# The last token group's second product: 26 block products instead of 28

## The chip, the cores and the metric

The kernel runs on one core of a Trainium2 chip. The metric is the device time of one execution in microseconds (us). A core has TensorE (PE, the matrix engine; PEld is its loading of weights), VectorE (DVE), ScalarE (ACT), GpSimd (POOL) and SyncE (SP, which issues transfers). Each works through a queue of its own in order and waits on semaphores for the others.

## The reference

Two stages, in float32. The first is an mLSTM cell over 4 batches, 8 heads, 768 steps and a head size of 40; its outcome is laid out as a matrix x of 3072 tokens by 320. The second, which the change touches, is

```
h = x @ w_in                    # 3072x320 @ 320x2048
g = np.maximum(0.01 * h, h)     # leaky relu
out = g @ w_out                 # 3072x2048 @ 2048x320
```

## The kernel before

**Stages.** The sequence is cut into 6 chunks of 128 steps. A chunk gives one token group: 4 blocks (one a batch) of 128 tokens. The loop at the end of the kernel goes over the groups; for each it runs a list of units that `ff_units` returns, and between them pieces of the cell for the next chunk. The order of issue on PE, DVE, ACT and POOL is the order in which the program is written. For the last group (g = 5) there is no cell work left: only its units run.

**First product.** `fast_firsts(g)` gives 14 units. They compute the transposed activations `acts` (2048 rows as 16 slices f of 128, by 512 tokens of the group) with a 2x2 scheme of Strassen's kind, 7 products for two values n each. A product is a set of matmuls with 64 weight rows and 256 columns at line 1036 into a pair of accumulator banks. For most units DVE then adds the pair of banks to `acts` (line 1065, 128x512 each), and ACT applies the leaky relu (line 1061). Units 8 to 13 in the last group finish with such a pair of adds.

**Second product.** `fast_units(g)` gives 14 units: again a 2x2 scheme with 7 products, once for each n of two. `acts` is seen as 2x2 blocks (two halves of the slices f, two token blocks), `w_out` as 2x2 blocks (two halves of the slices, two halves of 160 columns). One block product is 8 matmuls, each with 128x128 of `acts` as weights and 128x160 of `w_out` moving, summed in one accumulator bank (line 929). Sums of `acts` are made in place on DVE (lines 950, 955, 969, 983; 128x1024 each). Sums of the weights were made once, early (lines 231 to 234): `t2`, `t3`, `t4` in the tile `raw`, and one in place, so that the second column half of `w_out`'s first 8 slices no longer holds `w_out` itself but its difference to the first half. The results are put together by copies on ACT (lines 951, 966, 974, 981), adds on POOL (lines 967, 975, 977) and adds on DVE (lines 959, 988, 993), and sent off by SP (line 95, called from `send`). In the last group two token blocks go out in halves of 160 columns, the others whole.

**Banks.** Accumulator banks come from two pools of 4, `psf` (tag "mm") and `psc` (tag "c"). Products of both stages take `psf` in turn; `psc` serves the cell and is idle in the last group.

Of the kernel before, what the change touches and what calls it, by code (L numbers as in the profile page):

```python
# [8 lines left out]
F32 = mybir.dt.float32  # L9
# [3 lines left out]
AF = mybir.ActivationFunctionType  # L13
ALU = mybir.AluOpType
# [4 lines left out]
def kernel(  # L19
# [26 lines left out]
    nc = tc.nc  # L46
    B, H, S, D = q.shape
    P = 128
    BH = B * H
    NB = S // P  # L50
    NS = B * NB
    Dm, FF = moe_w_in.shape
    PR = H // 2
    DP = 64
    D1 = D + 1
# [24 lines left out]
    wk = ctx.enter_context(tc.tile_pool(name="wk", bufs=2))  # L80
    psf = ctx.enter_context(tc.tile_pool(name="psf", bufs=4, space=PSUM))
    psc = ctx.enter_context(tc.tile_pool(name="psc", bufs=4, space=PSUM))
# [18 lines left out]
    sync, by_act = queues = Ordered(nc.sync), Ordered(nc.scalar)  # L101
# [37 lines left out]
    NL = 4  # L139
    NR = 2  # L140
    EAB = 2
    kn = consts.tile([P, NL, H, DP], F32, name="kn")
    qn = consts.tile([P, NL, H, DP], F32, name="qn")
    S_t = [consts.tile([P, 2, H, DP], F32, name=f"S{n}") for n in range(NL)]
    S_v = [t[:].rearrange("p u h (k d) -> p u h k d", d=QW) for t in S_t]
    rb_t = [consts.tile([P, 3, RW], F32, name=f"rb{n}") for n in range(NR)]
    xb = consts.tile([P, PR * TB, QW], F32, name="xb")
    w_all = consts.tile([P, NL, H * P], F32, name="w")
    acts = consts.tile([P, NF, GT], F32, name="acts")
# [41 lines left out]
    QN = NF // 4  # L191
    QC = 4 * P
    WC = KC * 2 * P
    w_in = consts.tile([P, QN, WC], F32, name="w_in")
    w_out = consts.tile([P, NF, Dm], F32, name="w_out")

    def f_of(r, j):
        n, e = divmod(j, 2)
        return 4 * n + 2 * r + e

    def w_row(r, slot, j):
        n, e = divmod(j, 2)
        at = (e * KC + slot) * P
        return w_in[DP * r : DP * (r + 1), n, at : at + P]
# [10 lines left out]
    raw_l = raw_t[:].bitcast(F32)  # L215
    KH = NF // 2
    NH = Dm // 2
    low_w, high_w = w_out[:, :KH, :], w_out[:, KH:, :]
# [6 lines left out]
    p1_at = [raw_l[:, at + 12 * P + 2 * HT + n * NH :][:, :NH] for n in range(2)]  # L225
# [640 lines left out]
    def ff_units(g):  # L866
        xT = st["xT", g]

        def rows(j, ph, cols, slots):
            for slot in slots:  # L870
                for r in range(2):
                    nc.tensor.matmul(  # L872
                        ph[r][:, cols], lhsT=w_row(r, slot, j), rhs=xT[DP * r : DP * (r + 1), slot, cols],
                        start=(slot == 0), stop=(slot == KC - 1),
                    )

        def relu(j, ph, cols):
            for r in range(2):
                f = f_of(r, j)
                nc.scalar.activation(acts[:, f, cols], ph[r][:, cols], AF.Prelu, alpha=0.01)  # L880

        def half(j, h):
            ph = [psf.tile([P, GT], F32, name=f"ph{r}", tag="mm") for r in range(2)]
            cols = ts(h, GT // 2)
            rows(j, ph, cols, range(KC))
            relu(j, ph, cols)

        po = {}

        def part(n, m):  # L890
            if m == 0:
                po[n] = psf.tile([P, Dm], F32, name="po", tag="mm")
            for f in range(m * NF // 4, (m + 1) * NF // 4):
                nc.tensor.matmul(  # L894
                    po[n][:], lhsT=acts[:, f, ts(n, P)], rhs=w_out[:, f, :], start=(f == 0), stop=(f == NF - 1),
                )
            if m == 3:
                if n < 2:
                    y = wk.tile([P, Dm], F32, name="y")[:]
                else:  # L900
                    y = wk.tile([P, H, D1], F32, name="hn")[:].rearrange("p h d -> p (h d)")[:, :Dm]
                nc.scalar.copy(y, po[n][:])
                sync.dma_start(out[n * S + g * P : n * S + (g + 1) * P, :], y)

        if g == 0:

            ins = [(j, h) for j0 in range(0, NF // 2, 4) for h in range(2) for j in range(j0, j0 + 4)]
            ins = ins[:2] + ins[4:6] + sorted(ins[2:4] + ins[6:])
            return [lambda j=j, h=h: half(j, h) for j, h in ins] + [
                lambda n=n, m=m: part((n + 2) % B if m == 3 else n, m) for m in range(4) for n in range(B)  # L910
            ]
        return fast_firsts(g) + fast_units(g)

    def quarter(n, i, k):

        return acts[:, k * KH : (k + 1) * KH, ts(2 * i + n, P)]

    def fast_units(g):


        t1 = low_w[:, :, NH:]
        t2, t3, t4 = t_at
        y = [[None, None], [None, None]]
        t = p1_at

        def product(n, left, right):
            bank = psf.tile([P, NH], F32, name="po", tag="mm")
            for f in range(KH):
                nc.tensor.matmul(bank[:], lhsT=left[:, f, :], rhs=right[:, f, :], start=f == 0, stop=f == KH - 1)  # L929
            return bank[:]  # L930

        def half(n, i, d):
            if y[i][n] is None:
                if i == 0:
                    y[i][n] = wk.tile([P, Dm], F32, name="y")[:]
                else:
                    y[i][n] = wk.tile([P, H, D1], F32, name="hn")[:].rearrange("p h d -> p (h d)")[:, :Dm]
            return y[i][n][:, ts(d, NH)]

        last = g == NB - 1  # L940

        def send(n, i, d=None):
            b = 2 * i + n
            cols = slice(0, Dm) if d is None else ts(d, NH)
            sync.dma_start(out[b * S + g * P : b * S + (g + 1) * P, cols], y[i][n][:, cols])

        def p1(n):
            got = product(n, quarter(n, 0, 0), low_w[:, :, :NH])
            s1 = quarter(n, 1, 0)
            nc.vector.tensor_tensor(s1, s1, quarter(n, 1, 1), op=ALU.add)  # L950
            nc.scalar.copy(t[n], got)
            if n == 1:
                for m in range(2):
                    s2 = quarter(m, 0, 0)
                    nc.vector.tensor_tensor(s2, quarter(m, 1, 0), s2, op=ALU.subtract)

        def p2(n):
            got = product(n, quarter(n, 0, 1), high_w[:, :, :NH])
            nc.vector.tensor_tensor(half(n, 0, 0), t[n], got, op=ALU.add)
            if last:  # L960
                send(n, 0, 0)

        def p6(n):
            got = product(n, quarter(n, 0, 0), t2)
            u2 = half(n, 0, 1)
            nc.scalar.copy(u2, got)  # L966
            nc.gpsimd.tensor_tensor(u2, u2, t[n], op=ALU.add)  # L967
            s4 = quarter(n, 0, 1)
            nc.vector.tensor_tensor(s4, s4, quarter(n, 0, 0), op=ALU.subtract)

        def p7(n):
            got = product(n, quarter(n, 1, 1), t3)
            u3 = half(n, 1, 1)
            nc.scalar.copy(u3, got)
            nc.gpsimd.tensor_tensor(u3, u3, half(n, 0, 1), op=ALU.add)
            c21 = half(n, 1, 0)
            nc.gpsimd.tensor_tensor(c21, c21, u3, op=ALU.add)

        def p4(n):
            got = product(n, quarter(n, 1, 1), t4)  # L980
            nc.scalar.copy(half(n, 1, 0), got)
            s3 = quarter(n, 1, 1)
            nc.vector.tensor_tensor(s3, s3, quarter(n, 0, 0), op=ALU.subtract)

        def p5(n):
            got = product(n, quarter(n, 1, 0), t1)
            for i in (1, 0):
                nc.vector.tensor_tensor(half(n, i, 1), half(n, i, 1), got, op=ALU.add)
            send(n, 1)

        def p3(n):
            got = product(n, quarter(n, 0, 1), high_w[:, :, NH:])
            nc.vector.tensor_tensor(half(n, 0, 1), half(n, 0, 1), got, op=ALU.add)
            send(n, 0, 1 if last else None)

        return [lambda p=p, n=n: p(n) for p in (p1, p2, p4, p6, p7, p5, p3) for n in range(2)]

    K1, K2, KX = slice(0, 2), slice(2, 4), 4
# [21 lines left out]
    def fast_firsts(g):  # L1020
# [90 lines left out]

        order = (p2, p1, p6, p7, p4, p5, p3) if swapped else (p1, p6, p7, p4, p2, p5, p3)
        return [lambda p=p, n=n: p(n) for p in order for n in range(2)]

    def u_gates(c):
        gates_T(c, bus.pop(c)[0])
# [67 lines left out]
    def first_chunk():  # L1184
# [58 lines left out]
        prepare_step(1)  # L1243
        run(e, 2)
        ffs = ff_units(0)
        u_transpose(2, (on_s, on_s))
        run(e, 4)
# [33 lines left out]
    with tc.manual_schedule(engines={E.PE, E.DVE, E.Activation, E.Pool}):  # L1281
# [33 lines left out]
        N1 = 14  # L1315
# [3 lines left out]
        for c in range(1, NB + 1):  # L1319
            if c > 1:  # L1320
                ffs = ff_units(c - 1)
# [117 lines left out]
```

## Time and profile before

| what | us |
|---|---|
| median of 3 runs | 473.98 (473.94 to 474.25) |
| the profiled execution | 473.84 |
| its span | 472.0 |
| first product of the last group | 407.1 to 438.4 |
| second product of the last group | 438.4 to 469.1 |
| last add and last store | 469.1 to 472.0 |

The profile shows one execution. The span runs from its first instruction to its last; 1.84 us of the measured time lie around it. Times within it are counted from its start. The granted clock of PE is 1.00 in all of it. A record at line 929 is half of a float32 matmul. In rows of the time line, "x2" merges two instructions that follow one another, the number ahead of the engine is the time that they cover together, and the bracket tells how long the engine sat idle before and what released it. The time of a single instruction is its duration from start to end; instructions of one engine can overlap at their ends.

### The profile page before, as it was taken

The page shows a single profiled execution, that of the slowest core. Times are in us where ns is not written, and L with a number is a line of the kernel's source. Part 1 is how long each engine was busy: PE and PEld are TensorE (multiplying, and loading weights), DVE is VectorE, ACT ScalarE, POOL GpSimd, SP SyncE. Part 2 cuts the span into 40 slices and gives each one's busy share as a digit, 9 for nine tenths or more (in the row PEclk, how much of TensorE's full clock was granted, in tenths as well). Part 3 has the DMA queues.
Part 4 walks back from the last instruction along what each step waited for, and adds up shares of the span by engine and source line. Part 5 has one row for each costly group of instructions (what it writes and reads, how often), then busy time and mean ns, then how long its engine had stood idle before and what let it go on. Part 6 is the DMA issues. An engine that isn't in the chain of part 4 may idle for free.

```text
span 472.0 us, 14167 instructions
## 1 busy us (share of the span) xinstructions
PE 463.1 (98%) x5716; PEld 416.3 (88%) x5716; DVE 336.8 (71%) x609; ACT 203.4 (43%) x497; POOL 171.7 (36%) x225
## 2 busy tenths in 40 slices
PE   9899999999999999999999999999999999999997
PEld 6677978777788999988999988999988999988997
DVE  5778688999479988867788867788847786104541
ACT  2657878755336511366311366311456311253210
POOL 4332377264335164923214923214822005300020
PEclk9999999999999999999999999999999999999999
DMA  9999998887732695865754865853875202100001
GB/s 130 169 192 187 188 205 220 206 181 145 153 110 65 159 166 112 176 153 129 171 119 106 181 130 126 198 114 79 188 151 124 74 9 81 58 0 2 8 8 42
DMA packets 160993, 59.21 MB, mean 125 GB/s; under 512 B 123808, under 2 KB 152352, under 8 KB 160928
## 3 DMA queue, kind: packets, MB, share of 16 engines
q1 hardware_dynamic: 120944, 51.15, 48.9%
q10 hardware_dynamic: 39984, 7.17, 9.4%
q8 instruction: 45, 0.74, 0.7%
q14 instruction: 20, 0.16, 0.1%
HBM read 51.58 MB, written 6.70 MB: 123 GB/s over the span
## 4 chain that ended last, share of the span: by engine, by line
PE 87%; SPq 5%; POOL 3%; issue 3%; DVE 1%; DMA 1%; ACT 0%; POOLq 0%
PE ph L1036 33%; PE po L929 33%; PE po L894 8%; SPq L95 5%; PE pT L813 3%; PE ph L872 3%; PE sd L725 3%; PE sd L731 1%; DMA raw<-in_o_gate_dram 1%; PE hN L785 1%; POOL w L537 1%; POOL y L576 1%; POOL S L701 1%; PE pa L760 0%; PE tk L638 0%
## 5 line engine op out<-in xcount | busy, mean ns | idle before, releaser
L929 PE MATMUL po<-w_out,acts 128*128 128x160 f32 x640 | 89.1, 300 | 0.0
L929 PEld LDWEIGHTS po<-w_out,acts 128*128 128x128 f32 x640 | 87.3, 190 | 0.6 <-ACT acts L1061 0.3
L1036 PE MATMUL ph<-xT,w_in 64*128 64x256 f32 x720 | 82.7, 378 | 0.0
L1036 PEld LDWEIGHTS ph<-xT,w_in 64*128 64x128 f32 x720 | 69.2, 187 | 8.6 <-issue 0.6
L1065 DVE TENSOR_TENSOR acts<-acts,ph 128x512 f32<-128x512 f32 x60 | 38.4, 683 | 40.7 <-PE ph L1036 40.6
L929 PE MATMUL po<-raw,acts 128*128 128x160 f32 x480 | 66.4, 300 | 0.0
L929 PEld LDWEIGHTS po<-raw,acts 128*128 128x128 f32 x480 | 65.4, 190 | 0.3
L537 POOL TENSOR_SCALAR_AFFINE_SELECT w<-w 64x512 f32<-64x512 f32 x40 | 34.0, 850 | 52.9 <-DMA w<-a_dr 51.7
L1069 ACT COPY acts<-ph 128x512 f32<-128x512 f32 x60 | 32.2, 588 | 48.8 <-PE ph L1036 48.8
L1061 ACT ACTIVATE acts<-acts 128x1024 f32<-128x1024 f32 x30 | 31.6, 1055 | 41.8 <-DVE acts L1065 32.4
L701 POOL TENSOR_TENSOR S<-S,f 40x336 f32<-40x336 f32 x36 | 30.6, 849 | 47.8 <-PE pT L813 32.1
L547 ACT ACTIVATE w<-w,gT 128x64 f32<-128x64 f32 x160 | 41.6, 337 | 11.7 <-DMA a_dr<-a 4.3
L742 DVE TENSOR_TENSOR qn<-w,sd 64x384 f32<-64x384 f32 (+1 forms) x80 | 33.4, 418 | 14.3 <-ACT acts L1069 8.4
L872 PE MATMUL ph<-xT,w_in 64*128 64x256 f32 x320 | 37.3, 381 | 0.9 <-issue 0.7
L894 PE MATMUL po<-w_out,acts 128*128 128x320 f32 x128 | 36.7, 437 | 0.0
L1036 PE MATMUL ph<-acts,w 64*128 64x256 f32 x320 | 36.3, 379 | 0.0
L827 POOL TENSOR_TENSOR xb<-xb,den 128x320 f32<-128x320 f32 x16 | 11.6, 727 | 67.0 <-DVE xb L824 64.7
L872 PEld LDWEIGHTS ph<-xT,w_in 64*128 64x128 f32 x320 | 31.9, 187 | 3.8 <-ACT w_out L303 0.9
L1036 PEld LDWEIGHTS ph<-acts,w 64*128 64x128 f32 x320 | 30.6, 187 | 3.6
L894 PEld LDWEIGHTS po<-w_out,acts 128*128 128x128 f32 x128 | 23.5, 190 | 9.2 <-ACT acts L880 0.3
L967 POOL TENSOR_TENSOR y<-y,raw 128x160 f32<-128x160 f32 x10 | 9.5, 950 | 59.5 <-ACT y L966 59.5
L612 DVE TENSOR_TENSOR qn<-kqT,ea 64x512 f32<-64x512 f32 x32 | 30.0, 939 | 0.8
(184 smaller groups left out, 732.2 us busy)
## 6 DMA issues: line engine op xcount, KB each, us to landing
rb<-in_k_dram SPq DMA_DIRECT2D x64, 80.0 KB
rb<-in_q_dram SPq DMA_DIRECT2D x64, 80.0 KB
rb<-in_o_gate_dram SPq DMA_DIRECT2D x64, 80.0 KB
ea<-a_dr SPq DMA_DIRECT2D x32, 128.0 KB
raw<-in_moe_w_out_dram SPq DMA_DIRECT2D x6, 640.0 KB
w<-a_dr ACTq DMA_DIRECT2D x24, 128.0 KB
x_dr<-x SPq DMA_DIRECT2D x64, 40.0 KB
xT<-x_dr SPq DMA_DIRECT2D x16, 160.0 KB
```

The costliest lines, as they stand in the source:

```text
L537: nc.gpsimd.affine_select(part, part, compare_op=ALU.is_ge, fill=-1e30, base=0, pattern=[[0, H], [1, SL]], channel_multiplier=-1,)
L547: yield nc.scalar.activation(w[:, h, :], w[:, h, :], AF.Exp, bias=gT[c][:, 0, bh : bh + 1], scale=1.0)
L612: nc.vector.tensor_tensor(mixed(s)[rows, 1 - r], d["kqT"][rows, 1].rearrange("p (h t) -> p h t", t=SL), d["ea"][rows], op=ALU.mult,)
L701: nc.gpsimd.tensor_tensor(new, old, g, op=ALU.mult)
L742: nc.vector.tensor_tensor(mixed(s)[toks, u, hs], w[toks, hs], bank[1 - u][to[u][hs.start], hs], op=ALU.mult,)
L872: nc.tensor.matmul(ph[r][:, cols], lhsT=w_row(r, slot, j), rhs=xT[DP * r : DP * (r + 1), slot, cols], start=(slot == 0), stop=(slot == KC ...
L894: nc.tensor.matmul(po[n][:], lhsT=acts[:, f, ts(n, P)], rhs=w_out[:, f, :], start=(f == 0), stop=(f == NF - 1),)
L929: nc.tensor.matmul(bank[:], lhsT=left[:, f, :], rhs=right[:, f, :], start=f == 0, stop=f == KH - 1)
L1036: nc.tensor.matmul(bank[r][:, e, :], lhsT=left(r)[rows, e], rhs=right(r)[rows], start=first and e == 0 and m == 0, stop=e == 1 and m == le ...
L1061: nc.scalar.activation(to, z, AF.Prelu, alpha=0.01)
L1065: nc.vector.tensor_tensor(to[:, 2 * r : 2 * r + 2], to[:, 2 * r : 2 * r + 2], bank[r], op=ALU.add)
L1069: nc.scalar.copy(to[:, 2 * r : 2 * r + 2], bank[r])
```

## The change

For the last group alone the second product follows another bilinear scheme. `acts` is taken as 4x4 blocks (4 token blocks by 4 quarters of the slices f, 128x512 each) and `w_out` as 4x2 blocks (4 quarters by 2 halves of the columns, 128x640 each). 26 products P0 to P25 replace the 28 of that partition (two schemes with 14 quarter-size products each, 14 products of double depth in the code). Each is 4 matmuls into one bank, even ones from `psc`, odd ones from `psf`.

- `LAST_EARLY` is worked off between the 14 units of the first product: after unit 0 the first 8 slices of `w_out` are restored in place (one DVE add of 128x1280), after units 0 to 7 come 18 sums of weight blocks B0 to B17, after units 8 to 12 the sums A0 to A4 of activation blocks, all on DVE.
- `LAST` is worked off afterwards, one line for each product: its 4 matmuls, then sums A for later products (DVE), copies of results (ACT, lines with a single term and "=") and updates of the outputs c and of sums N (DVE, "+=" and "-="). In all 23 sums A, 36 updates and 18 copies.
- Sums lie in tiles that nothing else uses any more (`raw`, `kn`, `qn`, the `rb` tiles, `w`, `S`, `xb`, and `w_in` once the first product is through).
- A token block is sent whole when both halves are done; token block 1 (rows c2) goes in halves and comes last.

```diff
+        if g == NB - 1:
+            return last_units(g, fast_firsts(g))
         return fast_firsts(g) + fast_units(g)
...
-        last = g == NB - 1
-
-        def send(n, i, d=None):
+        def send(n, i):
...
-            if last:
-                send(n, 0, 0)
...
-            send(n, 0, 1 if last else None)
+            send(n, 0)
...
+    LAST_ROWS, LAST_KS = (0, 2, 1, 3), (1, 2, 0, 3)
+    LAST_EARLY = {
+        0: "B0 = b10 - b11",
+        1: "B1 = b21 + B0; B2 = b00 + b30",
...
+        8: "A0 = a01 - a21",
+        9: "A1 = a21 + a23",
+        10: "A2 = a01 - A1",
+        11: "A3 = a11 + a31",
+        12: "A4 = a13 + A3",
+    }
+    LAST = (
+        "P0 = A0 * B4",
+        "P1 = A1 * B11; A5 = a33 + A4; c20 = P0",
+        "P2 = a31 * b10; A6 = a00 + A2; c21 = P1; A7 = a10 - a12; N0 = P1",
+        "P3 = A2 * B8; A8 = A6 - a30; c30 = P2; N1 = -P2; A9 = a02 - a32",
+        "P4 = a13 * B17; A10 = A7 - a32",
+        "P5 = A4 * B10; N0 -= P3; c10 = -P4; A11 = a10 - A10",
+        "P6 = A5 * b31; A12 = a00 - a03; N1 += P5",
+        "P7 = A8 * B2; A13 = A12 - a30; N2 = N1; c31 = P6; c10 += N1",
...
+        "P10 = A13 * B9; A17 = A15 - a32; N5 = -P9; A18 = A10 + A12",
...
+        "P22 = A22 * B0; N7 += P19; A27 = a22 + A26",
+        "P23 = A23 * B3; c00 += N7; c30 += N7; c20 += P20",
+        "P24 = A25 * b20; N8 -= P20; c30 += P21; N9 = P23; c21 -= N8; N2 -= P22",
+        "P25 = A27 * b21; N9 += N8; c11 = N2; c31 -= N2; c10 += N9; c11 += N9; c20 -= P24; c21 += P25",
+    )
+
+    def last_units(g, firsts):
...
+        def send(w):
+            m, d = LAST_ROWS[int(w[1])], int(w[2])
+            if w[:2] != "c2":
+                whole.add(w)
+                if {w[:2] + "0", w[:2] + "1"} - whole:
+                    return
+                cols = slice(0, Dm)
+            else:
+                cols = ts(d, NH)
+            sync.dma_start(out[m * S + g * P : m * S + (g + 1) * P, cols], rows[m][:, cols])
+
+        def do(line):
+            to, op, *ws = line.split()
+            signed, ws = ws[0], [w.strip("-") for w in ws if w not in ("+", "-", "*")]
+            src = [name(w) for w in ws]
+            if op == "=" and " * " in line:
+                bank = name(to)
+                for f in range(4):
+                    nc.tensor.matmul(bank, lhsT=src[0][:, f, :], rhs=src[1][:, f, :], start=f == 0, stop=f == 3)
+            elif len(src) == 2:
+                nc.vector.tensor_tensor(name(to), src[0], src[1], op=ALU.add if " + " in line else ALU.subtract)
+            elif op == "=":
+                if signed[0] == "-":
+                    nc.scalar.activation(name(to), src[0], AF.Copy, scale=-1.0)
+                else:
+                    nc.scalar.copy(name(to), src[0])
+            else:
+                z = name(to)
+                nc.vector.tensor_tensor(z, z, src[0], op=ALU.add if op[0] == "+" else ALU.subtract)
+            used(to, *ws)
...
+        def ahead_of(n):
+            firsts[n]()
+            if n == 0:
+                nc.vector.tensor_tensor(low_w[:, :, NH:], low_w[:, :, NH:], low_w[:, :, :NH], op=ALU.add)
+            if n in LAST_EARLY:
+                run_lines(LAST_EARLY[n])
```

More of the change, by code (lines that the diff above doesn't have):

```diff
@@ L938, in half @@
             return y[i][n][:, ts(d, NH)]
-        last = g == NB - 1
-        def send(n, i, d=None):
+        def send(n, i):
             b = 2 * i + n
-            cols = slice(0, Dm) if d is None else ts(d, NH)
-            sync.dma_start(out[b * S + g * P : b * S + (g + 1) * P, cols], y[i][n][:, cols])
+            sync.dma_start(out[b * S + g * P : b * S + (g + 1) * P, :], y[i][n])
         def p1(n):
@@ L1113, in fast_firsts, with name, used, run_lines @@
         return [lambda p=p, n=n: p(n) for p in order for n in range(2)]
+    LAST_ROWS, LAST_KS = (0, 2, 1, 3), (1, 2, 0, 3)
+    LAST_EARLY = {
[13 rows of a table added]
+    }
+    LAST = (
[26 rows of a table added]
+    )
+    def last_units(g, firsts):
+        lo = raw_l[:, : 3 * KH * NH]
+        rows = [wk.tile([P, Dm], F32, name="y")[:] for _ in range(2)]
+        rows += [wk.tile([P, H, D1], F32, name="hn")[:].rearrange("p h d -> p (h d)")[:, :Dm] for _ in range(2)]
+        NW, AW = 4 * NH, 4 * P
+        flat = [t[:].rearrange("p n h d -> p (n h d)") for t in (kn, qn)]
+        flat += [t[:].rearrange("p u h d -> p (u h d)") for t in S_t]
+        r_l = [t[:].rearrange("p u w -> p (u w)") for t in rb_t]
+        sums_b = [lo[:, n * NW : (n + 1) * NW] for n in range(6)]
+        sums_b += [t[:, n * NW : (n + 1) * NW] for t in flat[:2] + r_l for n in range(3)]
+        sums_b += [t[:, :NW] for t in flat[2:]]
+        sums_a = [w_all[:, n, :AW] for n in range(NL)] + [t[:, :AW] for t in sums_b[18:]]
+        del sums_b[18:]
+        sums_a += [xb[:].rearrange("p n d -> p (n d)")]
+        sums_c = [t[:, NW + n * NH :][:, :NH] for t in flat[2:] for n in range(2)] + p1_at
+        behind = [w_all[:, n, AW:] for n in range(NL)]
+        behind += [w_in[:, n, m * AW : (m + 1) * AW] for n in range(QN) for m in range(2)]
+        text = "; ".join([LAST_EARLY[n] for n in sorted(LAST_EARLY)] + list(LAST))
+        words = [w.strip("-") for w in text.replace(";", " ").split()]
+        left = {w: words.count(w) for w in words}
+        spare = {"A": sums_a, "B": sums_b, "N": sums_c}
+        tiles = {}
+        def name(w):
+            kind, rest = w[0], w[1:]
+            if w in tiles:
+                return tiles[w]
+            if kind == "a":
+                m, n = LAST_ROWS[int(rest[0])], LAST_KS[int(rest[1])]
+                return acts[:, 4 * n : 4 * n + 4, ts(m, P)]
+            if kind == "b":
+                n = LAST_KS[int(rest[0])]
+                return w_out[:, 4 * n : 4 * n + 4, ts(int(rest[1]), NH)]
+            if kind == "c":
+                m = LAST_ROWS[int(rest[0])]
+                return rows[m][:, ts(int(rest[1]), NH)]
+            if kind == "P":
+                pool, tag = ((psc, "c"), (psf, "mm"))[int(rest) % 2]
+                tiles[w] = pool.tile([P, NH], F32, name="pl", tag=tag)[:]
+            else:
+                got = spare[kind].pop(0)
+                tiles[w] = got if kind == "N" else got.rearrange("p (f d) -> p f d", f=4)
+            return tiles[w]
+        def used(*ws):
+            for w in ws:
+                left[w] -= 1
+                if left[w] == 0 and w[0] == "A":
+                    spare["A"].append(tiles[w].rearrange("p f d -> p (f d)"))
+                if left[w] == 0 and w[0] == "N":
+                    spare["N"].append(tiles[w])
+                if left[w] == 0 and w[0] == "c":
+                    send(w)
+        whole = set()
+        def send(w):
[23 more added lines that the diff above has]
+                    nc.scalar.copy(name(to), src[0])
+            else:
+                z = name(to)
+                nc.vector.tensor_tensor(z, z, src[0], op=ALU.add if op[0] == "+" else ALU.subtract)
+            used(to, *ws)
+        def run_lines(lines):
+            for line in lines.split(";"):
+                do(line.strip())
+        def ahead_of(n):
[4 more added lines that the diff above has]
+                run_lines(LAST_EARLY[n])
+        def product(n):
+            if n == 0:
+                sums_a.extend(behind)
+            run_lines(LAST[n])
+        return [lambda n=n: ahead_of(n) for n in range(len(firsts))] + [lambda n=n: product(n) for n in range(len(LAST))]
```

19 rows, old and new, of tables (LAST, LAST_EARLY) are left out of this document.

## The prediction

> **What bounds the kernel.** I read the page first (busy shares, granted clock), then the chain that ended last for its final stretch, then the time line of that stretch on every engine, then a table of windows.
>
> ```profile
> span 472.0 us, 14167 instructions
> PE 463.1 (98%) x5716; PEld 416.3 (88%) x5716; DVE 336.8 (71%) x609; ACT 203.4 (43%) x497; POOL 171.7 (36%) x225
> ...
> PEclk9999999999999999999999999999999999999999
> ...
> PE 87%; SPq 5%; POOL 3%; issue 3%; DVE 1%; DMA 1%; ACT 0%; POOLq 0%
> ```
>
> TensorE (PE) is busy 98% of the span at full granted clock. An average does not price one stage, so here is the end of the chain that ended last (start, length, what):
>
> ```profile
> 429.83 8.63 PE ph L1036 x80
> 438.46 30.64 PE po L929 x224
> 469.10 0.02 issue
> 469.12 0.32 DVE y L993
> ```
>
> The last group's second product is one unbroken run of 224 records at line 929 (two for each matmul); behind it come one VectorE (DVE) add and the last store. So the stage is worth what its records are worth, as long as nothing else ends later. The busy times of the engines, in four windows (first half and second half of the first product; the second product; the tail; columns PE, PEld, DVE, ACT, POOL), show who could:
>
> ```profile
> 407.10:422.70 15.60, 15.60 (x145) 14.02 (x146) 0.32 (x1) 7.53 (x14) 0.00 (x0) 1.00 0.03 12
> 422.70:438.40 15.70, 15.70 (x148) 13.79 (x145) 6.43 (x10) 6.37 (x7) 0.00 (x0) 1.00 0.01 2
> 438.40:469.10 30.70, 30.68 (x226) 30.44 (x224) 12.62 (x17) 3.40 (x9) 3.95 (x6) 1.00 0.06 20
> 469.10:472.00 2.90, 0.00 (x0) 0.00 (x0) 0.32 (x1) 0.00 (x0) 0.00 (x0) 1.00 0.09 28
> ```
>
> DVE does next to nothing in the first window, 6.43 us in the second and 12.62 us of 30.70 in the third. The change lives on that room.
>
> **The change part by part.** The issue order of after is that of before on every engine, with the same waits, up to the last group's first product; there the 288 records of line 1036 stay the same. All differences lie after 407 us.
>
> *Products.* Removed: 14 products of 8 matmuls. Added: 26 of 4. That is 112 against 104 matmuls of the same form (128x128 weights, 160 columns), 224 against 208 records. What one costs in the stream, from the time line: the copy of the first product starts at 440.92 and the add behind the last at 469.12, 13 products of 16 records between, so 28.20/13 = 2.169 us each and 135.6 ns a record. Saved: 16 x 135.6 ns = **2.17 us**. Could closing a group of 4 instead of 8 cost more? The nearest row is line 894, where groups of 4 matmuls follow one another: 16 records take 4.47 us and 8 take 2.32, a difference of 2.15 for 8, or 269 ns, and inside 8 it is (2.32 - 0.43)/7 = 270. No cost at the border; I take 0. The first product of before took 2.42 us (438.46 to 440.88), 0.25 more than the rest; the wait row puts 0.33 of idle ahead of it down to ScalarE (ACT). The new first product waits for nothing new, but the switch from 64-row to 128-row tiles stays. Gain 0 to 0.3 us; I take 0, as an idle of 0.17 also stands where the tiles switch the other way at 407.11.
>
> *DVE while the first product runs.* Added: one add of 128x1280 that restores the second column half of w_out's first 8 slices (1.45 us, line 232's row of that size) and 18 sums of weight blocks, 128x640. These lines give the price; the bracket is DVE's idle time ahead:
>
> ```profile
> 425.61 1.28 DVE L1065 TENSOR_TENSOR acts<-acts,ph 128x512 f32<-128x512 f32 x2 [18.07 <-PE ph L1036]
> ...
> 440.90 2.36 DVE L950 TENSOR_TENSOR acts<-acts 128x1024 f32<-128x1024 f32 x2 [1.12 <-ACT acts L1061]
> 443.18 2.35 DVE L955 TENSOR_TENSOR acts<-acts 128x1024 f32<-128x1024 f32 x2
> ...
> 462.66 0.32 DVE L988 TENSOR_TENSOR hn<-hn,po 128x160 f32<-128x160 f32 x1 [7.43 <-POOL hn L977]
> 462.90 0.31 DVE L988 TENSOR_TENSOR y<-y,po 128x160 f32<-128x160 f32 x1
> ```
>
> Two adds of 512 elements, 683 ns each, are done in 1.28, so the second starts 0.60 after the first. Two pairs of 1024 start 2.28 apart, 1.14 an add. Two of 160 start 0.24 apart. So an add holds DVE for its elements at 1.04 ns plus some 0.07 us, and lasts 0.15 longer than its elements. For 640 elements: 0.74 held, 0.81 alone. Sum: 1.45 + 18 x 0.74 + 0.2 (two read the result just ahead of them) = 15.0 us; with none overlapping, 1.45 + 18 x 0.81 = 16.1. The idle time is 18.07 us, so 2 to 3 us are left, and line 1065's adds (in after, line 1062) start when they did. Without that cover each us late would hold back the leaky relu and the banks of the last first-product units. Cost 0. The 5 sums of activations behind units 8 to 12 (128x512, 0.68) fall into gaps between pairs of adds of which the smallest is 0.93: cost 0.
>
> *DVE while the second product runs.* Removed: 8 sums of 1024 and 10 adds of 160 (12.6 us). Added: 23 sums of 512 and 36 updates of 160. Held: 23 x 0.60 + 36 x 0.235 = **22.3 us**. It starts at 439.80 (end of the last pair of line 1065, whose own place is unchanged), and PE would end at 438.71 + 26 x 1.085 = 466.9: room for 27.1 us. I walked the queue in order, each update waiting for its product, each sum for its terms. None of the 59 reads what the instruction ahead of it wrote. The smallest distance from a sum's end to the start of the product that reads it is 3.3 us (A13 for P10); the sums A25 and A27 of the last two products are ready 4.0 and 3.6 us early. DVE idles at its waits for some 4.8 us, last before the add of P25. So the products go on unbroken, and after the last one 0.32 us of DVE remain, as before. Cost 0, if the held times are right; it is the weakest step. Queued behind each waiting update are sums for later products; that distance of 3.3 us is what such a wait could eat.
>
> *A rule of the Trainium skill against this step.* The pairs above show that a second add starts before the first has ended: 1.28 us for two of 0.683. The Trainium skill (VectorE: DVE Perf Modes, section The DRAIN you can't avoid) says instead that after an instruction the pipe must empty before the next one starts. By that rule the 59 would hold DVE for the sum of their durations and end about when PE does, at the same 471.8, with no room left for any gap between them.
>
> *ACT and POOL.* 18 copies of 160 (0.29 each, line 951's row) are 5.3 us of 28 on ACT, instead of 8. POOL's six adds go. All 8 accumulator banks are used in turn, so product n needs the readers of product n-8 done, which the walk has 3 us or more ahead. Cost 0.
>
> *Stores.* Before, 80 KB stores leave at 467.3 and 469.5, and 160 KB ones at 463.0 and 465.2. In after SP issues row block 3 (160 KB) about 1.2 us before PE ends, block 2 (160 KB) 0.7, half of block 1 (80 KB) 0.4 before, the last 80 KB 0.35 after. An issue takes SP 0.33, so none queues. A 160 KB store moved about 159 KB in 466.0 to 466.5 (317 GB/s), about 0.8 after its issue, so 400 KB need 1.3 us and are through about when the last store starts to move. Cost 0 to 0.4; I take 0.
>
> **Sum.** -2.17 us and nothing else. The profiled execution took 473.84 (span 472.0 and 1.84 around it): 471.67 by that. The median of the runs shown, 473.98, lies 0.14 above it: **471.8 us**.
>
> **Rivals.** (1) *DVE takes the full time of each instruction and a gap.* Chains on DVE show 0.04 between one's end and the next one's start where a result is passed on (385.08 to 385.12 at lines 820 and 749). If all 59 pay their duration and 0.04, the queue is 23 x 0.683 + 36 x 0.318 + 59 x 0.04 = 29.5 us from 439.80: it ends at 469.3 against 469.44 before, products unbroken, the gain given back behind the last product: 473.8. For it: many of the new instructions carry waits, which the pairs above had none or few of. Against it: line 955 waits for DVE too and started 0.08 before the end of line 950's last. Chance 0.08. The Trainium skill's page named above (VectorE: DVE Perf Modes) would lead here, once such a gap is added to its rule.
>
> (2) *DVE becomes the bound: slower.* Place: the same queue. It decides from a mean of 0.52 us an instruction (30.6 us for 59), 0.06 above full durations; above it sums are late for products too. A hand-over costs up to 0.14 in this trace (ACT's end at 458.54 to POOL's start at 458.68). With 0.10 on every duration the queue is 27.2 (durations alone) + 5.9 = 33.1 us and ends at 472.9 or later, 3.4 after DVE's end of before: 477.4. Against it: that gap is another engine's, and no DVE row in this stretch shows 0.10. Chance 0.11.
>
> (3) *Part of the gain is lost*: DVE ends up to 0.7 late through two-wait instructions, or the stores collide in full (0.4): 472.2 to 473.0. Chance 0.08. That the change doesn't do what it says is no rival: 26 groups of 4 stand in the issue order.
>
> **How the numbers follow.** Forecast 0.73, own range 471.3 (0.3 at the start and 0.2 of spread) to 472.2. With (3) that is 0.81 up to 473.0, so the range is 471.3 to 473.0. A difference of 0.2% (0.95 us) is about what a measurement of this kernel can tell from no change. Faster by more: 0.73 + 0.08 = 0.81; within: 0.08, from (1); slower: 0.11, from (2).
>
> **What would show it.** Right: 208 records of the new product line in one run of 28.2 to 28.5 us with no idle ahead of PE, DVE idle before its last add, the first pair of line 1062's adds still at 425.6. Wrong: a wait of PE for DVE in the last 30 us, a row of DVE updates without gaps that runs past PE's end, or 160-element updates starting more than 0.4 us apart while work is waiting.

## The result and the profile after

The changed kernel takes 471.96 us (median of 11 runs, 470.55 to 474.0) against 474.06 (median of 11, 473.31 to 477.32) beside it. The ratio is 0.9945 with a 95% interval of 0.9924 to 0.9966: faster by 1.6 to 3.6 us. The forecast was 471.8 and -2.17 us. The medians differ by 2.10.

The runs of one kernel scatter by more than the gain, so the stage is better read in the traces. Here is the end of the chain of after (start, length, what):

```profile
407.42 31.28 PE ph L1033 x288
438.70 28.46 PE pl L1236 x208
467.17 0.02 issue
467.19 0.32 DVE y L1246
```

Line 1033 is line 1036 of before, line 1236 is the new product. The first product takes 31.28 us, as before (407.18 to 438.46 there). The second is one run of 208 records in 28.46 us where 224 took 30.64. From the start of the first product to the end of the last one (the second product's P25) it is 59.75 against 61.92: **2.17 us less**. The tail behind it is 470.2 - 467.17 = 3.03 against 2.90, 0.13 more, and the first product starts 0.24 later, for reasons ahead of the change. The windows answer to those of before (columns PE, PEld, DVE, ACT, POOL):

```profile
407.35:422.90 15.55, 15.55 (x145) 13.98 (x146) 15.14 (x20) 7.54 (x14) 0.00 (x0) 1.00 0.03 12
422.90:438.65 15.75, 15.75 (x149) 13.85 (x145) 9.44 (x15) 6.37 (x7) 0.00 (x0) 1.00 0.00 1
438.65:467.17 28.52, 28.50 (x210) 28.26 (x208) 23.99 (x60) 6.02 (x19) 0.00 (x0) 1.00 0.03 11
467.17:470.20 3.03, 0.00 (x0) 0.00 (x0) 0.32 (x1) 0.00 (x0) 0.00 (x0) 1.00 0.37 124
```

DVE has become nearly full: 15.14 us where it had 0.32, 23.99 of 28.52 where it had 12.62 of 30.70. PE is busy in every window all the same. The time line of DVE shows that both covers held:

```profile
425.85 1.28 DVE L1062 TENSOR_TENSOR acts<-acts,ph 128x512 f32<-128x512 f32 x2 [3.19 <-PE ph L1033]
...
447.81 1.29 DVE L1238 TENSOR_TENSOR w_in<-w_in,acts 128x512 f32<-128x512 f32 x2
449.01 0.68 DVE L1238 TENSOR_TENSOR w_in<-w 128x512 f32<-128x512 f32 x1
...
467.19 0.32 DVE L1246 TENSOR_TENSOR y<-y,pl 128x160 f32<-128x160 f32 x1 [0.53 <-PE pl L1236]
```

The first adds of line 1062 still start 18.50 us behind the first product's start, with 3.19 us of idle time ahead. Three sums of 512 start 0.60 apart. Ahead of the last add DVE waits 0.53 for PE. The sums A13, A25 and A27 end 3.2, 3.8 and 3.5 us ahead of the products that read them (446.44 against 449.60, 460.98 against 464.82, 462.41 against 465.90); 3.3, 4.0 and 3.6 were forecast.

### The profile page after: what moved, and what is told of

Same layout as the page of the kernel before. It is cut to its first block, busy times and chain, and to the rows that moved or that the text cites. A ratio compares the mean times of both kernels' runs of the same rounds, so it can differ in the third digit from the quotient of the medians.

```text
span 470.2 us, 14195 instructions
## 1 busy us (share of the span) xinstructions
PE 459.6 (98%) x5700; PEld 412.5 (88%) x5700; DVE 365.4 (78%) x676; ACT 206.6 (44%) x507; POOL 170.1 (36%) x219
## 4 chain that ended last, share of the span: by engine, by line
PE 88%; DMA 5%; SPq 3%; POOL 1%; issue 1%; ACT 0%; DVE 0%; POOLq 0%; DVEq 0%
PE ph L1033 33%; PE po L931 26%; PE po L894 8%; PE pl L1236 6%; PE pT L813 3%; SPq L95 3%; PE ph L872 3%; PE sd L725 3%; DMA kn<-in_k_dram 3%; DMA acts<-in_moe_w_in_dram 1%; DMA w<-a_dr 1%; PE sd L731 1%; PE tk L638 1%; PE hN L785 1%; PE tkq L652 0%
## 5 line engine op out<-in xcount | busy, mean ns | idle before, releaser
L931 PE MATMUL po<-w_out,acts 128*128 128x160 f32 x512 | 71.3, 300 | 0.0
L931 PEld LDWEIGHTS po<-w_out,acts 128*128 128x128 f32 x512 | 69.9, 190 | 0.3
L931 PE MATMUL po<-raw,acts 128*128 128x160 f32 x384 | 53.2, 300 | 0.0
L931 PEld LDWEIGHTS po<-raw,acts 128*128 128x128 f32 x384 | 52.3, 190 | 0.3
L894 PEld LDWEIGHTS po<-w_out,acts 128*128 128x128 f32 x128 | 23.5, 190 | 9.2 <-ACT acts L880 0.3
L1033 PE MATMUL ph<-xT,raw 64*128 64x256 f32 x240 | 26.8, 376 | 0.0
```

The costliest lines, as they stand in the source:

```text
L894: nc.tensor.matmul(po[n][:], lhsT=acts[:, f, ts(n, P)], rhs=w_out[:, f, :], start=(f == 0), stop=(f == NF - 1),)
L1033: nc.tensor.matmul(bank[r][:, e, :], lhsT=left(r)[rows, e], rhs=right(r)[rows], start=first and e == 0 and m == 0, stop=e == 1 and m == le ...
```

## The experiments

Each is the changed kernel with one edit. Diffs are cut with `...` where lines or their ends are left out. Since all that runs before 400 us is the same code, the trace gives a second measure beside the time: from the start of the first product to the end of the last product (59.75 us in after, 61.92 in before), and the tail behind that.

**Two products more.**

```diff
-        "P8 = A9 * B6; A14 = a10 + a20; ...
+        "P8 = A9 * B6; P26 = a00 * b00; A14 = a10 + a20; ...
-        "P17 = A16 * B16; N3 += N6; ...
+        "P17 = A16 * B16; P27 = a01 * b10; N3 += N6; ...
```

> Two products more, each 4 matmuls on blocks that are there anyway (P26 behind P8, P27 behind P17); nobody reads their banks, the output is unchanged. Theory (the gain is 16 records of PE, a group of 4 matmuls costs half a group of 8, everything else is covered): PE's run of the second product grows from 28.47 to 30.64 us, 2.17 more, and the time comes back to that of before within 0.2 us. Rival (DVE or the stores already cost something behind the products): DVE gets 2.2 us more room, so less than 2.17 is lost, 1.5 to 1.9. Rival (a group costs something of its own, 40 ns each): 30.64 would be passed by 0.1 and the first product of before would not be 0.25 longer by the switch alone.

Measured: ratio to before 0.9991 (0.9976 to 1.0006), 474.34 us against 474.62; the profiled executions are 0.10 apart (473.74 and 473.84). The chain:

```profile
407.00 31.28 PE ph L1033 x288
438.28 30.64 PE pl L1236 x224
```

28 groups of 4 matmuls take 30.64 us, to the hundredth what 14 groups of 8 took. So the gain in the products is 16 records and nothing else, and a group border costs nothing. Both rivals fall.

**No sums in the second product.**

```diff
         def do(line):
             to, op, *ws = line.split()
+            if to[0] == "A" and int(to[1:]) > 4:
+                return
...
```

The lines left out let the products read A0 to A4 and keep the tiles of these from being given out again.

> The 23 sums A5 to A27 on DVE in the second product are left out (the products read A0 to A4 in their place, the output is not the reference's); products, updates, copies and stores stay. Theory (DVE is covered): time from the first product's start to the end of the last product stays 59.8 us and the tail 3.0, the whole within 0.2 us of the changed kernel. Rival (DVE costs part of the gain): 0.2 to 0.7 us less.

Measured: 59.75 us (407.25 to 467.00) and a tail of 3.0; the time is 472.61, ratio 0.9961 (0.9942 to 0.9980). The median is 0.65 above that of after, more than the 0.2 expected, but well inside the scatter; the profiled executions are 0.17 apart (471.79 and 471.96). With 23 of DVE's 59 instructions gone the products take the same time and the tail is as long: DVE costs nothing of the gain.

**More load for DVE in the second product**, 16 and 50 idle adds of 160:

```diff
             run_lines(LAST[n])
+            for m in range(1 if 4 <= n < 20 else 0):   # dve16; dve50: 2 if n < 25 else 0
+                pads = [w_in[:, i, 8 * P : 8 * P + NH] for i in range(QN)]
+                nc.vector.tensor_tensor(pads[m % 2], pads[2], pads[3], op=ALU.add)
```

> 16 idle adds of 128x160 more on DVE, one behind each of the products 4 to 19, 3.8 us at 0.235 each; output unchanged. Theory (4.8 us of DVE's time are free): no product waits, DVE still idles before the last add, the time stays that of the changed kernel within 0.2 us. Rival (the queue is full, every instruction pays its duration and a gap): 16 x 0.36 = 5.8 us later, less what is free.

> 50 idle adds of 128x160 more on DVE, two behind each of the products 0 to 24, 11.75 us at 0.235 each; output unchanged. Theory (4.8 us free, then DVE is the bound): DVE's queue is 34.0 us long; the walk of the queue gives 3.7 us of waits of PE for sums, DVE's end at 474.1 instead of 467.5, so the time is 6.6 us above the changed kernel, about 478.5. Rival (more free than the walk says): 0 to 4 us above it. Rival (every add pays 0.36): 18 us more queue, 13 us above it.

Measured with 16: 28.46 us for the products, no wait of PE, 0.53 of idle ahead of DVE's last add; 472.23 us, ratio 0.9948 (0.9929 to 0.9968). (The profiled execution of this one reached the first product at 409.97, 2.6 us late, so only the median is compared with other runs.) With 50: 479.31 us, ratio 1.0112 (1.0085 to 1.0138), 7.4 above after by the medians and 6.4 by the profiled executions (478.34 to 471.96). Of its four runs the two slower ones (479.88 and 480.82) have a mean granted clock of 0.984 and 0.985, the two faster ones 0.996. PE's time line shows where the time goes:

```profile
463.05 1.25 PE L1236 MATMUL pl<-raw,S 128*128 128x160 f32 x8
466.58 1.35 PE L1236 MATMUL pl<-w_out,xb 128*128 128x160 f32 x8 [2.28 <-DVE xb L1238]
468.96 1.35 PE L1236 MATMUL pl<-w_out,w_in 128*128 128x160 f32 x8 [1.02 <-DVE w_in L1238]
```

PE waits 2.28 + 1.02 = 3.3 us for the sums of the last two products (3.7 expected), and DVE ends at 473.36, 35.4 us behind the second product's first record at 437.96; the walk had 474.1, 35.5 us behind 438.63, where that record stands in after. In after DVE ends 28.9 us behind that record, so 11.75 us of load moved its end by 6.5: some 5.2 us were free, where the walk had 4.8. Below the edge (3.8 us in dve16) the load costs nothing; what lies above it delays the end. Where the edge lies between the two runs rests on the walk.

**More load while the first product runs**, 4 and 18 weight sums made twice:

```diff
             if n in LAST_EARLY:
                 run_lines(LAST_EARLY[n])
+            if n in (1, 2):                  # b_four; b_twice: n < 8
+                run_lines(LAST_EARLY[n])
```

> The weight sums B1 to B4 are made twice (4 adds of 128x640 more, 3.0 us at 0.74 each), while the first product runs; output unchanged. Theory (3.19 us of DVE's idle time were left ahead of the first adds of line 1062): those adds start where they did, within 0.1 us of 18.5 us behind the first product's start, time as the changed kernel. Rival (the cover is less than the idle time shown): each us that is missing shows as a wait of PE.

> All 18 weight sums are made twice (13.3 us more, 10.1 above the idle time that was left); output unchanged. Theory: the first adds of line 1062 come 10.1 us late; PE has units 8 and 9 in their banks by then and waits for a free bank ahead of unit 10, for 8.5 to 9 us; the time grows by as much, to about 480.7. Rival (the banks give more room, or later work is drawn together): 0 to 5 us.

Measured with 4: the adds start at 425.65 behind a first product that starts at 407.15, with 0.24 us of idle time left of 3.19; 59.75 us, 471.75, ratio 0.9940 (0.9906 to 0.9975). The cover is what the idle time shows. With 18: ratio 1.0191 (1.0144 to 1.0238), 483.97 us in two runs, 3.3 more than expected. PE waits 8.47 us ahead of unit 10, as the theory has it. But it runs slowly afterwards (columns from the left: window, its length, PE, PEld, DVE, ACT, POOL, granted clock):

```profile
428.70:431.00 2.30, 0.03 (x2) 0.00 (x0) 2.27 (x4) 0.00 (x0) 0.00 (x0) 0.99 0.00 0
431.00:434.00 3.00, 0.00 (x0) 0.00 (x0) 3.00 (x5) 0.00 (x0) 0.00 (x0) 0.50 0.00 0
434.00:437.10 3.10, 0.00 (x0) 0.00 (x0) 3.10 (x6) 0.00 (x0) 0.00 (x0) 0.50 0.00 0
437.10:439.00 1.90, 1.80 (x7) 1.70 (x9) 1.90 (x5) 1.06 (x1) 0.00 (x0) 0.50 0.00 0
439.00:441.00 2.00, 2.00 (x13) 2.00 (x11) 1.14 (x2) 1.06 (x1) 0.00 (x0) 0.50 0.00 0
441.00:443.00 2.00, 2.00 (x20) 2.00 (x19) 0.96 (x2) 0.00 (x0) 0.00 (x0) 0.96 0.00 0
```

The granted clock falls to 0.50 some 2.2 us after PE went idle (428.73) and stays there until about 4 us after it resumed. The 96 records of units 10 to 13 take 12.87 us; at the undisturbed rate (31.28/288) they take 10.43. So an idle time of 8.5 us costs 2.4 more behind it; half the clock for 4 us is 2.0 of that, the rest is open. The Trainium skill (TensorE: Matmul & The Clock Gate, section What's actually happening) describes such a gate, with a window of about 3.4 us of activity or idleness; the way back took 3.9 us here (437.2 to 441.1), the fall came sooner than that, 2.2 us after the last record.

**POOL busy beside it, and the sums on POOL.**

```diff
# pool_busy, in product(n), behind run_lines(LAST[n])
+            for m in range(2 if n < 20 else 0):
+                pads = [w_in[:, i, 8 * P : 10 * P] for i in range(QN)]
+                nc.gpsimd.tensor_tensor(pads[m], pads[2], pads[3], op=ALU.add)
# sums_pool, in do()
-                nc.vector.tensor_tensor(name(to), src[0], src[1], ...
+                eng = nc.gpsimd if to[0] == "A" and int(to[1:]) > 4 else nc.vector
+                eng.tensor_tensor(name(to), src[0], src[1], ...
```

> 40 idle adds of 128x256 on POOL, two behind each of the products 0 to 19 (some 0.75 us each, 30 us); output unchanged. In before a pair of DVE adds of 1024 took 2.67 us instead of 2.36 where one POOL add of 160 lay beside it, and that add 0.90 or 1.33 instead of 0.52. Reading 1 (the two engines take turns at their SBUF operands, each loses what the other one uses): DVE loses 0.3 to 0.5 us for each POOL add that meets one of its own, 12 to 20 us for 40; less 4.8 us free the changed kernel gets 5 to 13 us slower (PE waits for sums). Reading 2 (DVE is only some 10% slower, as the means 1345 against 1220 ns have it): queue 24 us, no change of time.

> The 23 sums A5 to A27 of the second product go to POOL instead of DVE; output unchanged. POOL's adds of 128x512 start 1.34 us apart (line 1018 of before), so 23 need 30.8 us from 440, and A27 is ready at 470.9 or later: PE waits for sums from P9 on, its end comes 5 us later than 467.1 if POOL runs free, up to 13 later if each of DVE's 36 updates also holds it up. So the time is 477 to 485. Rival (POOL would have covered it too): as the changed kernel.

Measured: 478.82 us with POOL busy, ratio 1.0085 (1.0058 to 1.0112), 6.9 above after: reading 1. POOL's adds start earlier than meant, with the first product still running, and run without a gap from 429.1 to 466.8. DVE's time line:

```profile
440.61 0.68 DVE L1238 TENSOR_TENSOR S<-acts,S 128x512 f32<-128x512 f32 x1
441.21 1.22 DVE L1238 TENSOR_TENSOR S<-acts,w 128x512 f32<-128x512 f32 x1
...
445.76 1.21 DVE L1238 TENSOR_TENSOR w<-S,acts 128x512 f32<-128x512 f32 x1
446.89 0.31 DVE L1246 TENSOR_TENSOR S<-S,pl 128x160 f32<-128x160 f32 x1
447.13 0.98 DVE L1238 TENSOR_TENSOR w<-acts,w 128x512 f32<-128x512 f32 x1
448.03 1.21 DVE L1238 TENSOR_TENSOR w<-acts 128x512 f32<-128x512 f32 x1
449.16 0.31 DVE L1246 TENSOR_TENSOR S<-S,pl 128x160 f32<-128x160 f32 x1
...
467.86 0.68 DVE L1238 TENSOR_TENSOR S<-w,w_in 128x512 f32<-128x512 f32 x1
```

A sum with two operands in SBUF (the core's main memory, where the tiles lie) takes 1.21 us instead of 0.68 where it follows another sum, and 0.98 where it follows an update; an update with one operand in an accumulator bank keeps its 0.31. The sum at 440.61 starts 0.01 ahead of a POOL add and keeps its 0.68; that add takes 1.26 instead of 0.73. From there on DVE's sums start 1.13 to 1.15 us apart, and so do POOL's adds (441.84, 442.98, 444.12): one of each in turn. At 467.86, with POOL through, a sum takes 0.68 again. In the other kernel POOL does the sums and only the updates with two SBUF operands (S<-S,S) are long:

```profile
457.02 1.39 DVE L1247 TENSOR_TENSOR S<-S,S 128x160 f32<-128x160 f32 x1
458.33 0.31 DVE L1247 TENSOR_TENSOR S<-S,pl 128x160 f32<-128x160 f32 x1
```

It takes 475.94 us, ratio 1.0031 (1.0007 to 1.0056), 4.0 above after and below the lower end of the 477 to 485 expected: POOL's sums started 1.3 us apart, but from 437.5 on instead of 440, so A27 was ready at 467.5 and PE waited only 0.35 and 1.29; the rest is DVE, which ends at 470.25, 1.3 behind the last product. The direction was right; the low end of what was expected was 1 us too high.

**The tail.** Three late stores left out, and two of them issued by another queue:

```diff
# tail_alone, in send()
+            if w != "c21" and w[:2] != "c0":
+                return
# tail_act, in send()
+            eng = nc.scalar if w[:2] in ("c1", "c3") else sync
```

> Three of the last stores are left out (token blocks 2 and 3, and the first half of block 1, so these parts of the output stay unwritten); the last 80 KB store leaves alone. Theory (400 KB issued in the 1.6 us ahead of it cost it next to nothing): from the last product's end to the end of the span 2.90 to 3.03 us. Rival (the stores collide): 2.90 as in before against 3.03 in the changed kernel, and less where more was lost.

> The stores of token blocks 2 and 3 are issued by ACT's queue instead of SP's; output unchanged. Theory (SP's issues of 0.33 us do not queue): tail 3.0 us, time as the changed kernel within 0.2 us. Rival (SP holds the last store up): 0.1 to 0.3 us less.

Measured: 469.9 - 466.96 = 2.94 us for the store that leaves alone (one execution), 469.0 - 465.99 = 3.01 with ACT's queue (ratio to before 0.9933, 0.9904 to 0.9962; 472.07 us, as after). The other traces of the changed products without extra load on DVE or POOL have tails of 2.98 to 3.03 us, so the 400 KB ahead of the last store cost at most 0.1 us. No run points to a kernel that beats the changed one beyond the scatter.

## Why the prediction was right, point by point

- **Products, 16 records of 135.6 ns.** Right: -2.18 in the chain (30.64 to 28.46), undone to the hundredth by two more products. No cost for borders: right.
- **The start of the first product.** The idle of 0.33 us of PEld, put down to ACT in before, stands in after too, with "issue" as its cause and no wait on the new first product. So it was not the wait for ACT, and taking 0 was right. It fits the switch from 64-row to 128-row tiles, which is in both kernels; no run leaves the switch out. The Trainium skill (TensorEngine Tiling (Array Packing), section Key Properties) says that a change of tiling mode drains TensorE; 0.33 us is the idle time that the trace shows at this change, 0.17 at the one at 407.35.
- **DVE under the first product.** Right: 18.50 us to the first adds, 3.19 us left (a little more than the 2 to 3 forecast), and b_four and b_twice lie on the two sides of the edge of the cover. The price beyond it was only half in the working: the clock adds to it.
- **DVE under the second product.** The weakest step was right. An instruction held DVE for 0.60 or 0.23 us (from its start to the next one's), sums were ready early, and DVE idled 0.53 us ahead of the last add. dve16 and dve50 put its limit near where the walk had it. Rivals (1) and (2), a gap behind every instruction, fall: their queues end at 469.3 or later, DVE's end was 467.51 with idle time before it, and updates that read a product's bank start 0.23 apart as well:

```profile
462.80 0.31 DVE L1246 TENSOR_TENSOR y<-y,pl 128x160 f32<-128x160 f32 x1
463.03 0.32 DVE L1246 TENSOR_TENSOR raw<-raw,pl 128x160 f32<-128x160 f32 x1
463.26 0.31 DVE L1246 TENSOR_TENSOR hn<-hn,pl 128x160 f32<-128x160 f32 x1
```

  The rule that was set against this step (the pipe must empty first) does not describe these instructions, each of which starts before the one ahead has ended. The prediction quoted it without its exception: the section of the Trainium skill that it names (VectorE: DVE Perf Modes, The DRAIN you can't avoid) adds that an instruction that is not held starts earlier.
- **Stores.** 0 was taken, inside a stated 0 to 0.4; the tail became 0.13 longer than before, and 0.1 of it goes with the stores ahead (tail_alone).
- **The sum.** 471.67 for the profiled execution against 471.96 measured. The difference of 0.29 is 0.24 of a later start, which the change does not touch, and 0.13 of tail, less 0.08 around the span. That the medians come as close as 471.96 and 471.8 is partly luck, as the 11 runs lie between 470.55 and 474.0. In the traces of kernels whose code is the same up to there, the first product of the last group starts between 406.2 and 410.0 us, a spread as wide as that of the times. In the latest of them, dve16, the granted clock was 0.50 from about 31 to 37 us, where all the other traces have 1.00; how much of its delay that made, and what else spreads the starts, is open.

One thing was missing in the working: POOL's six adds were only counted as gone. In before, one of them took 1.33 us instead of 0.52 beside DVE's sums, which kept their time:

```profile
452.88 2.35 DVE L969 TENSOR_TENSOR acts<-acts 128x1024 f32<-128x1024 f32 x2
454.28 1.33 POOL L967 TENSOR_TENSOR y<-y,raw 128x160 f32<-128x160 f32 x1 [49.00 <-ACT y L966]
```

There it was POOL that waited, and it had time. With DVE nearly full, a POOL that works beside it takes the gain away, as pool_busy shows: that POOL is empty in this stage is a condition of the gain.

## What to carry to other kernels

Where one engine runs without a gap, fewer instructions of it are worth their spacing in the stream, here to the hundredth of a us, as long as the engines that feed it keep up. To know whether they do, walk their queues in order and count what an instruction holds its engine for (the distance of two starts), not how long it lasts. The room of the feeding engine is a budget with a sharp edge: under it more work is free, above it what is added shows in the time, and behind a long wait the matrix engine's clock takes its share. Before sums are moved to a second engine, check that the two do not take turns at the same operands.

## What the runs showed of the hardware

DVE and POOL took turns when both read two operands in SBUF: in pool_busy a 128x512 float32 add on DVE took up to 1.22 us instead of 0.68 beside POOL adds of 128x256, in sums_pool a 128x160 add up to 1.42 instead of 0.32 beside POOL adds of 128x512. The one that came first kept its time. With one operand in an accumulator bank DVE's add kept 0.31. The Trainium skill (SBUF — State Buffer, section Who interferes with whom) says so: a DVE instruction with two SBUF inputs contends with a GpSimd one that reads SBUF, and one with a single SBUF input does not; the runs agree. In dve50, PE idle for 2.3 and 1.0 us kept its full clock; in pool_busy, after a wait of 2.8 us in the time line, the clock was 0.50 and the last product took 2.34 us instead of 1.25. The moment of the fall is not fixed by the length of the wait alone: in b_twice it came 2.2 us after the last record, in pool_busy some 3.5 us (467.10 to 470.56), with PE already at work again. What sets it was not tried.
